# A running maximum, sums and an accumulator of its own for the ninth token set of a soft mixture of experts, and masks kept once

## The chip, the cores and the metric

The kernel runs on 1 core of one Trainium2 chip. The metric is the device time of an execution in microseconds; three runs of the kernel before gave 246.71, 247.36 and 250.5 us, with a median of 247.36 us. PE is the matrix engine (PEld its weight loads), DVE the vector engine, ACT the scalar engine, POOL the GpSimd engine, SP the engine that issues nearly all DMAs.

## The reference

Two parts follow each other. First comes attention over 8 batches, 8 heads, 576 positions and 64 columns per head. Heads 0 to 3 see the last 32 positions ("local"), heads 4 to 7 see every 32nd position ("strided"); the softmax subtracts the row maximum. The result is laid out as `x`, 4608 tokens of 512 columns. Then comes a soft mixture of experts with 8 experts of 4 slots:

```python
logits = x @ phi                                  # 4608 x 32
d = exp(logits - logits.max(0)); d /= d.sum(0) + 1e-9     # over all tokens
slot_input = d.T @ x                              # 32 x 512
slot_out[e] = relu(slot_input[e] @ w1[e]) @ w2[e]
c = exp(logits - logits.max(1)); c /= c.sum(1) + 1e-9     # over the 32 slots
out = c @ slot_out
```

The maximum, the sum and `d.T @ x` over all tokens are built up while attention runs, as running values that are rescaled whenever the maximum moves.

## The kernel before, in words

**Steps.** The work is cut into 16 iterations `i`, one for half the heads of a batch (`i // 2` is the batch). Each iteration takes the same steps, each a small function `emit_...`, named by a short key: scores (SL, SS), masking (a1, aA, a2), maximum and exponential (m, b, EX, s), transposes of the weights (PA, PL, PS), values (AL, AS, AA), normalising (nL, nS, nA), transposes of the result (XL, XS, XB), logits (LG, lc, lg). A table `PHASE` gives each key a time within the iteration, and the sorted list of all times is the order in which the program is written, and so the order on every engine. Keys that end in z stand for the last iteration. Weight loads are sorted into the same list: each takes a buffer when the step that last uses it has been written, and SP issues all loads in that order.

**Sets of tokens.** Tokens 64 to 575 of a batch form one set of 512 tokens, so there are eight sets, one per batch. Logits of such a set are kept as 128 partitions x 128 columns in `lall[:, b, :]`: partition 32 t + slot holds that slot for the t-th quarter of the tokens. Tokens 0 to 63 of all batches form the ninth set. Every fourth iteration (i = 3, 7, 11, 15) has 128 of its tokens together, and writes them to `lall[32 g : 32 g + 32, 8, :]` with g = i // 4.

**The ninth set before.** T9 transposes its 128 tokens (four transposes), x9 copies them, G9 (L577) makes the logits with four matmuls into the 32 partitions of quarter g, c9 copies them to `lall`, b9 takes their maximum, and `first_m9`, `last_m9` fold it into the running negative maximum that all sets share. E9 (L624) takes the exponential on 32 partitions, with the shared maximum; z9 adds its sums to the shared sums `z`. U9 transposes the 32 x 128 result, u9 copies it, and S9 (L675) multiplies it with the tokens: one matmul of 512 columns into the 32 partitions of quarter g of the same PSUM bank that the eighth-part sums SI have just been written to. `ac` (L680) then folds the whole bank into `acc`. In the last iteration SI, S9 and ac are done in two halves of 256 columns.

**The merge.** After the last iteration the four quarters are put together: mt transposes the maximum, gm takes the minimum of the four, wP, wD, wA make a factor per partition, sw scales the stacking matrix, sP (L759) multiplies the accumulator with it, sD (L766) copies the result to `sit`, the slot inputs that the first layer reads. zD, zP, rg make the reciprocal of the sum, which scales the hidden layer. The steps P0 to P6 (`emit_first`, L846) are the first layer and issue weight loads whose buffers it frees. The second layer (`emit_l2`, L944), the coefficients and the output follow.

**Banks.** `take` gives the PSUM bank that has been free the longest, `give` returns it; a step that takes a bank waits until its last reader is done. Engines that touch the same bank are put in order by the program.

**Masks.** `cb` holds the masks of nine score tiles side by side as bf16: four copies of the local mask, one for the first 64 tokens, four copies of the strided mask; 464 columns in all. One DMA at the start (L891) loads it.

Of the kernel before, what the change touches and what calls it, by code (L numbers as in the profile page):

```python
# [50 lines left out]
    lgz=492.0681, c9z=467.7215, bmz=518.3122, zzz=648.0242, z9z=668.8573, dtz=596.2488, EX1z=195.9649, EX2z=170.4399,  # L51
    fAz=234.7687, fLz=274.1149, fSz=217.6755, xLz=423.1816, xSz=473.4095, xBz=528.5387, x9z=397.8597, EDz=528.5407,
    E9z=609.9016, EAz=644.5397, b9=25.0188, U9=26.2638, u9=26.7833, b9z=480.3923, U9z=628.15, u9z=652.4228,
# [44 lines left out]
def tile_sparse_attention_soft_moe(  # L98
# [24 lines left out]
    WM = 320 + 4 * NI  # L123
    cb = big("cb", WM, BF16)
    mask = cb[:, 0:WM]
# [4 lines left out]
    acc = big("acc", 512)  # L130
    d = big("d", 128)
# [156 lines left out]

    def done(name, i, readers):
# [124 lines left out]
    def emit_a(w, i):  # L414

        if i not in box:
            box[i] = [state.tile([P, 9, 2], F32, tag=nm, name=f"{nm}{i}", bufs=4) for nm in ("mx", "rz")]
        s, n, kk, lo, t = {"1": (0, 4, 64, 0, "M1"), "A": (4, 1, 64, 0, "M2"), "2": (5, 4, NI, 128, "M2")}[w]
        dst = psg[2] if w == "2" else psg[1][:, s:s + n]
        mk = mask[:, 320:WM] if w == "2" else mask[:, 64 * s:64 * s + 64 * n]  # L420
# [80 lines left out]
    def emit_nA(i):  # L501
        t, rz = box.pop(("AA", i)), box[i][1]
        r0 = 64 * (i // 2 % 2)
        if i == NQ - 1:
            first_m9(i)
# [71 lines left out]
    def emit_G9(i):  # L577
        t = box["G9", i] = take()
        for c in range(4):
            nc.tensor.matmul(out=t[0][rows9(i), 0:128], lhsT=phs[:, CH[c], :], rhs=xT9(i)[:, c, :],  # L580
                             start=c == 0, stop=c == 3, skip_group_check=True)

    def emit_c9(i):
        r = rows9(i)
        t = box.pop(("G9", i))
        DVE(out=woven(lall[r, B, :]), in_=t[0][r, 0:128].rearrange("p (y k) -> p y k", y=2))
        give(t)

    def first_m9(i):
        st["m9", i] = state.tile([P, 1], F32, tag="m9", name=f"m9_{i}")  # L590
        DVE(out=st["m9", i], in_=st["m", i - 2])

    def emit_b9(i):

        r = rows9(i)
        bm9 = st["bm9", i] = state.tile([P, 1], F32, tag="bm", name=f"bm9_{i}")
        nc.vector.tensor_reduce(out=bm9[r], in_=lall[r, B, :], op=ALU.max, axis=AX.X)
        if i < NQ - 1:
            first_m9(i)
            last_m9(i)  # L600

    def last_m9(i):
        r = rows9(i)
        nc.vector.scalar_tensor_tensor(out=st["m9", i][r], in0=st["bm9", i][r], scalar=-1.0, in1=st["m", i - 2][r], op0=ALU.mult, op1=ALU.min)

    def emit_bm(i):
        b = i // 2
        bm = state.tile([P, 1], F32, tag="bm", name=f"bm{b}")
        nc.vector.tensor_reduce(out=bm, in_=lall[:, b, :], op=ALU.max, axis=AX.X)
        if i == NQ - 1:  # L610
            last_m9(i)

        ngm = st["m", i] = state.tile([P, 1], F32, tag="ngm", name=f"ngm{b}")
        if b == 0:
            nc.vector.tensor_scalar_mul(ngm, bm, -1.0)
        else:
            nc.vector.scalar_tensor_tensor(out=ngm, in0=bm, scalar=-1.0, in1=st["m9" if b % 2 else "m", i if b % 2 else i - 2], op0=ALU.mult, op1=ALU.min)

    def emit_ED(i):
        b = i // 2  # L620
        st["z", i] = state.tile([P, 1], F32, tag="zs", name=f"zs{b}")
        nc.scalar.activation(out=d, in_=lall[:, b, :], func=AF.Exp, bias=st["m", i], accum_out=st["z", i])

    def emit_E9(i):  # L624
        r = rows9(i)
        st["z9", i] = state.tile([P, 1], F32, tag="z9", name=f"z9_{i}")
        nc.scalar.activation(out=d9[r].rearrange("p (y k) -> p y k", y=2), in_=woven(lall[r, B, :]), func=AF.Exp, bias=st["m", i][r], accum_out=st["z9", i][r])
# [11 lines left out]
    def emit_z9(i):  # L639
        r = rows9(i)  # L640
        nc.vector.tensor_tensor(out=st["z", i][r], in0=st["z", i][r], in1=st["z9", i][r], op=ALU.add)
# [10 lines left out]
    def emit_U9(i):  # L652
        t = box["U9", i] = take()
        r = rows9(i)
        nc.tensor.transpose(out=t[0][:, 0:32], in_=d9[r], identity=ident[r, r])
# [19 lines left out]
    def emit_S9(i, hs=(0, 1)):  # L675
        cols = slice(256 * hs[0], 256 * hs[-1] + 256)
        nc.tensor.matmul(out=box["SI", i, hs[0]][0][rows9(i), cols], lhsT=dt9,
                         rhs=x9b[:, cols], start=False, stop=True, skip_group_check=True)
# [22 lines left out]
    for s in "LS":  # L701
# [9 lines left out]
               S9=emit_S9, ac=emit_ac)  # L711
    EVEN, ODD, FOURTH = {"lc", "Dt", "Tt", "et"}, {"lg", "bm", "ED", "EA", "DT", "dt", "SI", "zz", "ac"}, {"T9", "x9", "G9", "c9", "b9", "E9", "z9", "U9", "u9", "S9"}
    HALVES = {"SI", "S9", "ac", "rc"}


    L = NQ - 1
    gm = phs[0:1]
    wg = state.tile([P, 1], F32, name="wg")
    zw = state.tile([P, 1], F32, name="zw")
    rg = state.tile([P, 1], F32, name="rg")  # L720
# [5 lines left out]
    def emit_mt():  # L726
        box["mrg"] = take()
        nc.tensor.transpose(out=box["mrg"][0][0:1, 0:128], in_=st["m", L], identity=ident)
# [9 lines left out]
    def emit_wD():  # L738
        nc.vector.tensor_tensor(out=wg, in0=box["mrg"][0][:, 128:129], in1=st["m", L], op=ALU.subtract)
# [4 lines left out]
    def emit_zD():  # L744
        nc.vector.tensor_tensor(out=zw, in0=st["z", L], in1=wg, op=ALU.mult)

    def emit_zP():
        nc.tensor.matmul(out=box["mrg"][0][:, 129:130], lhsT=same, rhs=zw, start=True, stop=True)

    def emit_rg():  # L750

        nc.vector.tensor_scalar_add(rg, box["mrg"][0][:, 129:130], EPS)
        give(box.pop("mrg"))
        nc.vector.reciprocal(rg, rg)

    def emit_sw():
        nc.vector.tensor_scalar_mul(stw, stack, wg)

    def emit_sP(h):  # L759
        t = box["sit", h] = take()  # L760
        for c in range(2):
            x = 2 * h + c
            nc.tensor.matmul(out=t[0][:, 32 * c:32 * c + 32], lhsT=acc[:, 128 * x:128 * x + 128], rhs=stw,
                             start=True, stop=True, skip_group_check=True)

    def emit_sD(h):  # L766
        t = box.pop(("sit", h))
        DVE(out=sit[:, 2 * h:2 * h + 2, :].rearrange("p c (e x) -> p c e x", x=36)[:, :, :, 0:4],
            in_=t[0][:, 0:64].rearrange("p (c e s) -> p c e s", c=2, e=E))
        give(t)  # L770
# [75 lines left out]
    def emit_first(n):  # L846
# [7 lines left out]
        if n == 1:  # L854
# [4 lines left out]
            "rg": emit_rg, "sw": emit_sw, "ms": lambda: nc.gpsimd.memset(sitb, 0.0), "Px": lambda: ph.append(take())}  # L859
    for h in range(2):  # L860
        once[f"SI{h}"] = lambda h=h: emit_SI(L, (h,))
        once[f"S9{h}"] = lambda h=h: emit_S9(L, (h,))
# [198 lines left out]
```

## Time and profile before

| what | value |
|---|---|
| median of the three runs | 247.36 us |
| the profiled execution | 247.0 us, its span 245.2 us |
| PE busy | 219.2 us, 89% of the span |
| DVE busy | 166.9 us, 68% |
| ACT busy | 155.3 us, 63% |
| POOL busy | 87.3 us, 36% |
| DMA | 72.79 MB, mean 297 GB/s |
| mean granted TensorE clock | 0.967 of full speed |

The profiled execution is 247.0 us long; its span, in which the trace has instructions, is 245.2 us, and 1.8 us lie around it. A line such as L677 is a line of the kernel. In the views, `x32` is a count of instructions. A float32 matmul appears as two PE instructions, a transpose as one.

### The profile page before, as it was taken

Reading aid. Unit: us, or ns where it says so; the run is one execution under the profiler, and the core shown is the slowest. Engines: PE = TensorE matmul, PEld = TensorE weight load, DVE = VectorE, ACT = ScalarE, POOL = GpSimd, SP = SyncE. Lnnn points to the kernel's source line nnn. Section 1 sums busy time; section 2 is a strip of 40 time slices with the busy share of each in tenths; the row PEclk is TensorE's granted clock in tenths of the full one; section 3 lists DMA queues with packets and bytes.
Section 4 is the critical chain, followed back from the end, with each engine's and each line's share of the span. In section 5 each row is a group of like instructions: output and inputs, shape, how many; then the busy total and the mean of one; then the engine's idle time right before and its main releaser. Section 6 shows DMA issues by size and latency. Waiting matters only on the chain.

```text
span 245.2 us, 9712 instructions
## 1 busy us (share of the span) xinstructions
PE 219.2 (89%) x3974; PEld 168.7 (69%) x3974; DVE 166.9 (68%) x378; ACT 155.3 (63%) x344; POOL 87.3 (36%) x187
## 2 busy tenths in 40 slices
PE   6879999999999899999999999997989999898600
PEld 2569889899788789879989988776743245455300
DVE  6077778888779788878998988699767330145800
ACT  2469869797878688797897888694451040134600
POOL 5731662752456177146436603843102000000000
PEclk9799999999999999999999999999999999999955
DMA  6978999999999799999899999796999999988997
GB/s 157 296 225 241 310 301 280 272 295 290 306 278 301 202 318 280 277 276 318 256 289 320 279 258 268 270 266 237 392 413 409 409 398 350 288 282 278 325 364 298
DMA packets 70188, 72.79 MB, mean 297 GB/s; under 512 B 33280, under 2 KB 60288, under 8 KB 70144
## 3 DMA queue, kind: packets, MB, share of 16 engines
q1 hardware_dynamic: 69184, 71.84, 92.4%
q8 instruction: 31, 0.51, 0.9%
q10 hardware_dynamic: 960, 0.33, 0.6%
q14 instruction: 13, 0.11, 0.2%
HBM read 62.72 MB, written 9.44 MB: 294 GB/s over the span
## 4 chain that ended last, share of the span: by engine, by line
PE 67%; DMA 13%; DVE 7%; issue 3%; ACT 2%; SPq 2%; DVEq 0%; ACTq 0%
PE bank L466 11%; PE bank L335 11%; PE bank L385 8%; PE bank L836 6%; PE bank L516 5%; DMA natb<-in_q_dram 5%; PE bank L458 4%; DMA wb<-in_moe_w_dram 4%; PE bank L952 3%; PE bank L671 3%; PE bank L547 3%; DMA natb<-in_k_dram 3%; PE bank L536 2%; PE bank L977 2%; DMA xnb<-in_k_dram 2%
## 5 line engine op out<-in xcount | busy, mean ns | idle before, releaser
L335 PE MATMUL bank<-cf,natb 128*128 128x128 f32 x276 | 40.1, 275 | 1.9 <-DMA natb<-in_q_dram 1.8
L335 PEld LDWEIGHTS bank<-cf,natb 128*128 128x128 f32 x276 | 31.5, 142 | 5.5 <-issue 2.6
L423 DVE TENSOR_TENSOR pb<-bank,cb 128x128 f32<-128x128 f32 (+2 forms) x48 | 22.6, 476 | 9.9 <-PE bank L385 8.4
L351 ACT COPY kLb<-bank 64x256 f32<-64x256 f32 x64 | 25.3, 395 | 3.2 <-PE bank L335 1.3
L496 DVE TENSOR_TENSOR xnb<-bank,rz 128x512 f32<-128x512 f32 (+1 forms) x33 | 21.9, 670 | 7.7 <-ACT ptb L462 2.9
L385 PE MATMUL bank<-kLb,qtb 128*32 128x128 f32 x576 | 24.6, 274 | 1.5 <-ACT kLb L351 0.8
L431 DVE TENSOR_TENSOR pb<-pb,mx 128x288 f32<-128x288 f32 (+1 forms) x32 | 23.1, 722 | 0.7
L428 DVE TENSOR_REDUCE mx<-pb 128x8 f32<-128x288 f32 (+1 forms) x32 | 22.1, 692 | 0.6
L325 POOL COPY vb<-vb 64x1024 f32<-64x1024 f32 x16 | 17.4, 1090 | 14.2 <-PE bank L466 9.8
L438 DVE TENSOR_REDUCE rz<-pb 128x8 f32<-128x288 f32 (+1 forms) x32 | 20.9, 681 | 2.3 <-ACT pb L435 2.0
L435 ACT ACTIVATE pb<-pb 128x288 f32<-128x288 f32 (+1 forms) x32 | 19.0, 598 | 5.5 <-DVE pb L431 5.2
L385 PEld LDWEIGHTS bank<-kLb,qtb 128*32 128x32 f32 x576 | 18.2, 110 | 3.7 <-issue 2.5
L462 ACT COPY ptb<-bank 128x512 f32<-128x512 f32 x32 | 18.8, 590 | 2.9 <-PE bank L458 2.5
L330 POOL COPY natb<-natb 128x512 f32<-128x512 f32 x15 | 9.2, 612 | 31.5 <-DMA natb<-in_q_dram 24.0
L359 ACT COPY kSb<-bank 64x512 f32<-64x512 f32 x32 | 18.6, 581 | 2.3 <-PE bank L335 1.9
L516 PE MATMUL bank<-cf,xnb 128*128 128x128 f32 x128 | 19.8, 278 | 0.1
L378 POOL COPY kLb<-qtb 64x64 f32<-64x64 f32 x32 | 8.6, 267 | 29.9 <-ACT qtb L370 26.4
L466 PE MATMUL bank<-vb,ptb 128*32 128x128 f32 x512 | 18.0, 273 | 0.5 <-issue 0.5
L326 POOL COPY vb<-vb 64x1024 f32<-64x1024 f32 x16 | 18.1, 1129 | 0.7
L458 PE MATMUL bank<-cf,pb 128*128 128x128 f32 x128 | 17.3, 274 | 0.9 <-ACT pb L435 0.8
L466 PE MATMUL bank<-vs,ptb 128*32 128x128 f32 x480 | 17.2, 276 | 0.4 <-ACT ptb L462 0.3
L382 POOL COPY kSb<-qtb 64x32 f32<-64x32 f32 x64 | 16.7, 261 | 2.2
(179 smaller groups left out, 465.9 us busy)
## 6 DMA issues: line engine op xcount, KB each, us to landing
wb<-in_moe_w_dram SPq DMA_DIRECT2D x48, 512.0 KB
natb<-in_q_dram SPq DMA_DIRECT2D x30, 256.0 KB
natb<-in_k_dram SPq DMA_DIRECT2D x30, 256.0 KB
vb<-in_v_dram SPq DMA_DIRECT2D x32, 144.0 KB
vs<-in_v_dram SPq DMA_DIRECT2D x30, 144.0 KB
out_dram<-wb SPq DMA_DIRECT2D x16, 256.0 KB
vb<-in_moe_w_dram SPq DMA_DIRECT2D x4, 512.0 KB
xnb<-in_moe_w_dram SPq DMA_DIRECT2D x3, 512.0 KB
```

The lines of the kernel that those rows point to most:

```text
L335: nc.tensor.transpose(out=t[0][:, 128 * n:128 * n + 128], in_=src[:, 128 * n:128 * n + 128], identity=ident)
L351: ACT(out=dst.rearrange("d (p j n) -> d p j n", j=2, n=2)[:, :, :, n], in_=t[0][64 * n:64 * n + 64].rearrange("d (h j p) -> d p j h", j=2, ...
L385: nc.tensor.matmul(out=t[0][32 * c:32 * c + 32, x:x + wd], lhsT=lhsT, rhs=rhs, start=True, stop=True, skip_group_check=True)
L423: nc.vector.tensor_tensor(out=dst, in0=src, in1=mk.rearrange("p (s k) -> p s k", s=n).unsqueeze(3).to_broadcast([P, n, kk, 2]), op=ALU.add)
L428: nc.vector.tensor_reduce(out=part(box[i][0], w), in_=psg[w].rearrange("p s k a -> p s a k"), op=ALU.max, axis=AX.X)
L431: nc.vector.tensor_tensor(out=psg[w], in0=psg[w], in1=over(box[i][0], w), op=ALU.subtract)
L435: nc.scalar.activation(out=t, in_=t, func=AF.Exp, scale=0.125)
L438: nc.vector.tensor_reduce(out=part(box[i][1], w), in_=psg[w].rearrange("p s k a -> p s a k"), op=ALU.add, axis=AX.X)
L458: nc.tensor.transpose(out=t[0][:, 128 * r:128 * r + 128], in_=pb[:, lo + 128 * r:lo + 128 * r + 128], identity=ident)
L466: nc.tensor.matmul(out=t[0][32 * c:32 * c + 32, 128 * r:128 * r + 128], lhsT=lhsT, rhs=rhs, start=True, stop=True, skip_group_check=True)
L496: nc.vector.tensor_tensor(out=xn[:, place(i, s), r0:r0 + nr].rearrange("p r (a d) -> p r a d", a=2), in0=t[0][:, 128 * r0:128 * r0 + 128 * ...
L516: nc.tensor.transpose(out=t[0][:, 128 * r:128 * r + 128], in_=xn[:, place(i, s), r, :], identity=ident)
```

## The change

The ninth set leaves the shared running values and gets its own: a negative maximum `m9`, sums `z9`, a factor `al9` and an accumulator `acc9` of 128 partitions x 128 columns.

- G9 makes the logits four times, into all four quarters of the bank: 16 matmuls in place of 4.
- b9 takes the maximum straight from the bank, on 128 partitions; E9 takes the exponential straight from the bank too; c9 still copies the 32 partitions to `lall`, and the bank is given back when both c9 and E9 are done. `first_m9` and `last_m9` are gone.
- U9 transposes 128 x 128 in place of 32 x 128.
- S9 takes a bank of its own and makes four matmuls of 128 columns, one per quarter, in place of one of 512 columns; the new step a9 folds it into `acc9`. L9 makes the factor `al9` by an exponential.
- In the last iteration E9, U9 and u9 come before the shared exponential ED, and S9, which was written between the two halves of SI, is written just after the transpose DT.
- In the merge, `mn` is the smaller of the two negative maxima; wD, wA, zD and zP work on two columns; rg has two more small steps; s9w scales the identity by the factor of the ninth set; s9P, written between the two halves of SI, multiplies `acc9` with it into the bank that both halves of sP now add to.
- The masks are kept once (164 columns in place of 464) and repeated by a stride of zero when a1 and a2 read them.

The diff, cut to its core:

```diff
-    ok = np.concatenate([ok_l] * 4 + [ok_a] + [ok_s] * 4, 1)
+    ok = np.concatenate([ok_l, ok_a, ok_s], 1)
...
-        nc.vector.tensor_tensor(out=dst, in0=src,
-                                in1=mk.rearrange("p (s k) -> p s k", s=n).unsqueeze(3).to_broadcast([P, n, kk, 2]), op=ALU.add)
+                                in1=masks[w].unsqueeze(1).unsqueeze(3).to_broadcast([P, n, kk, 2]), op=ALU.add)
...
     def emit_G9(i):
         for c in range(4):
-            nc.tensor.matmul(out=t[0][rows9(i), 0:128], lhsT=phs[:, CH[c], :], rhs=xT9(i)[:, c, :],
+            for f in range(4):
+                nc.tensor.matmul(out=t[0][32 * f:32 * f + 32, 0:128], lhsT=phs[:, CH[c], :], rhs=xT9(i)[:, c, :],
...
     def emit_b9(i):
+        nc.vector.tensor_reduce(out=bm9, in_=box["G9", i][0][:, 0:128], op=ALU.max, axis=AX.X)
+        nc.vector.scalar_tensor_tensor(out=ng, in0=bm9, scalar=-1.0, in1=st["m9", i - 4], op0=ALU.mult, op1=ALU.min)
...
     def emit_bm(i):
+        if i == L:
+            nc.vector.tensor_tensor(out=mn, in0=ngm, in1=st["m9", i], op=ALU.min)
...
     def emit_E9(i):
+        nc.scalar.activation(out=d9, in_=box["G9", i][0][:, 0:128], func=AF.Exp, bias=st["m9", i], accum_out=st["z9", i])
+        done("G9", i, 2)
+    def emit_L9(i):
+        if i > 3:
+            nc.scalar.activation(out=st["al9", i], in_=st["m9", i - 4], func=AF.Exp, bias=st["m9", i], scale=-1.0)
...
-        nc.tensor.transpose(out=t[0][:, 0:32], in_=d9[r], identity=ident[r, r])
+        nc.tensor.transpose(out=t[0][:, 0:128], in_=d9, identity=ident)
...
-    def emit_S9(i, hs=(0, 1)):
-        nc.tensor.matmul(out=box["SI", i, hs[0]][0][rows9(i), cols], lhsT=dt9,
-                         rhs=x9b[:, cols], start=False, stop=True, skip_group_check=True)
+    def emit_S9(i):
+        t = box["S9", i] = take()
+        for f in range(4):
+            nc.tensor.matmul(out=t[0][32 * f:32 * f + 32, 0:128], lhsT=dt9, rhs=x9b[:, 128 * f:128 * f + 128], ...)
+    def emit_a9(i):
+            nc.vector.scalar_tensor_tensor(out=acc9, in0=acc9, scalar=st["al9", i], in1=t[0][:, 0:128], op0=ALU.mult, op1=ALU.add)
...
+    def emit_s9w():
+        nc.vector.tensor_scalar_mul(d9, ident, wg[:, 1:2])
+    def emit_s9P():
+        t = box["sit"] = take()
+        nc.tensor.matmul(out=t[0][:, 0:128], lhsT=acc9, rhs=d9, start=True, stop=False, skip_group_check=True)
     def emit_sP(h):
-        t = box["sit", h] = take()
+        for x in (2 * h, 2 * h + 1):
+            nc.tensor.matmul(out=box["sit"][0][:, 32 * x:32 * x + 32], lhsT=acc[:, 128 * x:128 * x + 128], rhs=stw,
+                             start=False, stop=True, skip_group_check=True)
```

The order of the changed steps in the last iteration, by engine:

```
PE  before: G9 LG XB mt DT wP U9 SI0 S9 SI1 S9 sP0 sP1 P0
PE  after:  G9 LG XB U9 mt DT S9 wP SI0 s9P SI1 sP0 sP1 P0
DVE before: c9 b9 lg bm(last_m9) gm dt wD zz u9 z9 sw ac0 ac1 sD0 sD1
DVE after:  b9 c9 lg bm(mn) u9 gm dt wD a9 zz z9 s9w sw ac0 ac1 sD0 sD1
ACT before: xS xB ED E9 EA wA
ACT after:  xS E9 xB ED EA L9 wA
```

## Rows read from the trace of the kernel before

**Rows 1.** Windows: us, busy us (instructions) per engine, granted clock, DMA share, GB/s.
```profile
20.00:156.00 136.00, 133.67 (x2803) 117.71 (x2805) 113.10 (x251) 112.22 (x252) 65.52 (x143) 1.00 0.96 281
...
171.00:214.00 43.00, 40.95 (x493) 20.69 (x489) 18.70 (x58) 12.00 (x29) 2.90 (x3) 1.00 1.02 383
```
**Rows 2.** The chain that ended last: start us, us, what.
```profile
36.38 0.87 PE bank L385 x32
...
156.05 5.81 DMA natb<-in_q_dram
...
200.90 8.79 DMA wb<-in_moe_w_dram
```
**Rows 3.** Who waited for whom: us in total, times, longest.
```profile
SPq L301 <- PE bank L335: 15.1, 10, 2.6
...
DVE x9b L508 <- PE bank L677: 2.5, 3, 1.0
...
PE bank L952 <- DMA wb<-in_moe_w_dram: 0.9, 1, 0.9
```
**Rows 4.** Window of the weight loads issued ahead of P0, columns as in Rows 1.
```profile
167.09:186.14 19.05, 17.07 (x242) 11.32 (x234) 14.96 (x44) 8.86 (x22) 3.39 (x3) 1.00 0.96 372
```
**Rows 5.** Timeline of SP in that window: first and last of 15 loads.
```profile
167.09 0.43 SPq L262 DMA_DIRECT2D kLb<-in_moe_w_dram  x1
...
181.79 1.24 SPq L256 DMA_DIRECT2D xnb<-in_moe_w_dram  x2
```
**Rows 6.** Timeline of PE around S9 of i = 3: start us, us, engine, line.
```profile
67.28 0.59 PE L677 MATMUL bank<-x9b,dt 128*32 128x512 f32 x1
67.29 0.42 PE L385 MATMUL bank<-kLb,qtb 128*32 128x128 f32 x6
67.71 0.59 PE L677 MATMUL bank<-x9b,dt 128*32 128x512 f32 x1
```
**Rows 7.** Timeline of PE around G9 and U9 of i = 7.
```profile
101.57 0.73 PE L580 MATMUL bank<-xnb,phs 128*32 128x128 f32 x5
...
102.25 0.31 PE L466 MATMUL bank<-vs,ptb 128*32 128x128 f32 x3
...
106.06 0.24 PE L655 MATMUL bank<-cf,d 32*128 32x32 f32 x1
106.23 0.66 PE L335 MATMUL bank<-cf,natb 128*128 128x128 f32 x4
```
**Rows 8.** Groups by form: busy us, mean ns of one | idle before, releasers.
```profile
L385 PEld LDWEIGHTS bank<-kLb,qtb 128*32 128x32 f32 x576 | 18.2, 110 | 3.7 <-issue 2.5 <-ACT kLb L351 1.1
...
L686 DVE SCALAR_TENSOR_TENSOR acc<-acc,al,bank 128x512 f32<-128x512 f32 x6 | 4.5, 746 | 0.2
...
L686 DVE SCALAR_TENSOR_TENSOR acc<-acc,al,bank 128x256 f32<-128x256 f32 x2 | 1.0, 480 | 0.6 <-PE bank L677 0.6
```
**Rows 9.** Timeline of the last iteration and the merge.
```profile
177.17 0.42 DVE L521 COPY xtb<-bank 128x256 f32<-128x256 f32 x1 [1.21 <-ACT xtb L521]
...
178.13 0.30 DVE L586 COPY lall<-bank 32x128 f32<-32x128 f32 x1 [0.54 <-PE bank L580]
...
179.16 0.59 ACT L540 COPY xnb<-bank 128x512 f32<-128x512 f32 x1 [0.77 <-PE bank L536]
...
179.79 0.40 ACT L622 ACTIVATE d<-lall,ngm 128x128 f32<-128x128 f32 x1
180.10 0.19 ACT L622 ACTIVATION_READ_ACCUMULATOR d<-lall,ngm 128x1 f32 x1
...
181.15 0.16 DVE L739 TENSOR_TENSOR wg<-bank,ngm 128x1 f32<-128x1 f32 x1
...
182.24 0.48 DVE L686 SCALAR_TENSOR_TENSOR acc<-acc,al,bank 128x256 f32<-128x256 f32 x1 [0.25 <-PE bank L677]
...
184.20 1.92 PE L836 MATMUL bank<-wb,pb 128*32 128x512 f32 x16
```
**Rows 10.** DMA issues: KB of one.
```profile
cb<-in_cb_dram ACTq DMA_DIRECT2D x1, 116.0 KB
```

More of the change, by code (lines that the diff above doesn't have):

```diff
@@ L121, in big @@
         return const.tile([P, cols], dt, name=nm)
-    WM = 320 + 4 * NI
+    WM = 128 + NI
     cb = big("cb", WM, BF16)
-    mask = cb[:, 0:WM]
+    masks = {"1": cb[:, 0:64], "A": cb[:, 64:128], "2": cb[:, 128:WM]}
     cf = big("cf", 128 + 128 + 32 + 1)
@@ L287, in tile_sparse_attention_soft_moe @@
     st = {}
+    L = NQ - 1
+    mm = state.tile([P, 2], F32, name="mm", bufs=1)
+    zz2 = state.tile([P, 2], F32, name="zz2", bufs=1)
+    mn = state.tile([P, 1], F32, name="mn", bufs=1)
     def done(name, i, readers):
@@ L579, in emit_G9 @@
         for c in range(4):
-            nc.tensor.matmul(out=t[0][rows9(i), 0:128], lhsT=phs[:, CH[c], :], rhs=xT9(i)[:, c, :],
-                             start=c == 0, stop=c == 3, skip_group_check=True)
+            for f in range(4):
+                nc.tensor.matmul(out=t[0][32 * f:32 * f + 32, 0:128], lhsT=phs[:, CH[c], :], rhs=xT9(i)[:, c, :],
+                                 start=c == 0, stop=c == 3, skip_group_check=True)
     def emit_c9(i):
         r = rows9(i)
[L585 to L591, printed above, removed]
-    def emit_b9(i):
[L595 to L604, printed above, removed]
+        DVE(out=woven(lall[r, B, :]), in_=box["G9", i][0][r, 0:128].rearrange("p (y k) -> p y k", y=2))
+        done("G9", i, 2)
+    def emit_b9(i):
+        bm9 = state.tile([P, 1], F32, tag="bm", name=f"bm9_{i}")
+        nc.vector.tensor_reduce(out=bm9, in_=box["G9", i][0][:, 0:128], op=ALU.max, axis=AX.X)
+        ng = st["m9", i] = mm[:, 1:2] if i == L else state.tile([P, 1], F32, tag="m9", name=f"m9_{i}")
+        if i == 3:
+            nc.vector.tensor_scalar_mul(ng, bm9, -1.0)
+        else:
+            nc.vector.scalar_tensor_tensor(out=ng, in0=bm9, scalar=-1.0, in1=st["m9", i - 4], op0=ALU.mult, op1=ALU.min)
     def emit_bm(i):
@@ L609, in emit_bm @@
         nc.vector.tensor_reduce(out=bm, in_=lall[:, b, :], op=ALU.max, axis=AX.X)
-        if i == NQ - 1:
-            last_m9(i)
-        ngm = st["m", i] = state.tile([P, 1], F32, tag="ngm", name=f"ngm{b}")
+        ngm = st["m", i] = mm[:, 0:1] if i == L else state.tile([P, 1], F32, tag="ngm", name=f"ngm{b}")
         if b == 0:
@@ L639, in emit_z9 @@
     def emit_z9(i):
[L640 to L641 removed]
+        if i > 3:
+            nc.vector.scalar_tensor_tensor(out=st["z9", i], in0=st["z9", i - 4], scalar=st["al9", i], in1=st["z9", i],
+                                           op0=ALU.mult, op1=ALU.add)
     def emit_DT(i):
@@ L727, in emit_mt @@
         box["mrg"] = take()
-        nc.tensor.transpose(out=box["mrg"][0][0:1, 0:128], in_=st["m", L], identity=ident)
+        nc.tensor.transpose(out=box["mrg"][0][0:1, 0:128], in_=mn, identity=ident)
     def emit_gm():
@@ L744, in emit_zD @@
     def emit_zD():
-        nc.vector.tensor_tensor(out=zw, in0=st["z", L], in1=wg, op=ALU.mult)
+        nc.vector.tensor_tensor(out=zw, in0=zz2, in1=wg, op=ALU.mult)
     def emit_zP():
-        nc.tensor.matmul(out=box["mrg"][0][:, 129:130], lhsT=same, rhs=zw, start=True, stop=True)
+        nc.tensor.matmul(out=box["mrg"][0][:, 129:131], lhsT=same, rhs=zw, start=True, stop=True)
     def emit_rg():
-        nc.vector.tensor_scalar_add(rg, box["mrg"][0][:, 129:130], EPS)
+        DVE(out=zw, in_=box["mrg"][0][:, 129:131])
         give(box.pop("mrg"))
+        nc.vector.scalar_tensor_tensor(out=rg, in0=zw[:, 1:2], scalar=0.25, in1=zw[:, 0:1], op0=ALU.mult, op1=ALU.add)
+        nc.vector.tensor_scalar_add(rg, rg, EPS)
         nc.vector.reciprocal(rg, rg)
     def emit_sw():
-        nc.vector.tensor_scalar_mul(stw, stack, wg)
-    def emit_sP(h):
-        t = box["sit", h] = take()
[L761 to L764, printed above, removed]
+        nc.vector.tensor_scalar_mul(stw, stack, wg[:, 0:1])
+    def emit_s9w():
[3 more added lines that the diff above has]
+        nc.tensor.matmul(out=t[0][:, 0:128], lhsT=acc9, rhs=d9, start=True, stop=False, skip_group_check=True)
+    def emit_sP(h):
+        for x in (2 * h, 2 * h + 1):
+            nc.tensor.matmul(out=box["sit"][0][:, 32 * x:32 * x + 32], lhsT=acc[:, 128 * x:128 * x + 128], rhs=stw,
+                             start=False, stop=True, skip_group_check=True)
     def emit_sD(h):
-        t = box.pop(("sit", h))
         DVE(out=sit[:, 2 * h:2 * h + 2, :].rearrange("p c (e x) -> p c e x", x=36)[:, :, :, 0:4],
-            in_=t[0][:, 0:64].rearrange("p (c e s) -> p c e s", c=2, e=E))
-        give(t)
+            in_=box["sit"][0][:, 64 * h:64 * h + 64].rearrange("p (c e s) -> p c e s", c=2, e=E))
+        if h:
+            give(box.pop("sit"))
     CSETS = ((0, 4), (4, 7), (7, NV))
@@ L858, in tile_sparse_attention_soft_moe @@
     once = {"zv": emit_zv, "mt": emit_mt, "gm": emit_gm, "wP": emit_wP, "wD": emit_wD, "wA": emit_wA, "zD": emit_zD, "zP": emit_zP,
-            "rg": emit_rg, "sw": emit_sw, "ms": lambda: nc.gpsimd.memset(sitb, 0.0), "Px": lambda: ph.append(take())}
+            "rg": emit_rg, "sw": emit_sw, "s9w": emit_s9w, "s9P": emit_s9P, "ms": lambda: nc.gpsimd.memset(sitb, 0.0), "Px": lambda: ph.append(take())}
     for h in range(2):
         once[f"SI{h}"] = lambda h=h: emit_SI(L, (h,))
-        once[f"S9{h}"] = lambda h=h: emit_S9(L, (h,))
         once[f"ac{h}"] = lambda h=h: emit_ac(L, (h,))
```

48 lines of the change are left out of this document (25 added, 23 removed).

## The prediction

> **What bounds the kernel now.** I read the windows first, to see which engine is full in which stretch. From 20 to 156 us, the attention loop, PE is busy 133.67 of 136 us and the DMA engines have a share of 0.96 [rows 1]: two resources are full at once, and DVE and ACT, at 113.1 and 112.2 us, have 17% to spare. From 171 to 214 us the DMA share is 1.02: the weights stream in without a gap. The chain of waits says how the two are coupled. In the loop it is nearly all PE; it then goes through a query load issued at 156.05 that lands 5.81 us later, and in the second layer through a weight load issued at 200.90 that takes 8.79 us [rows 2]. The list of waits says which way the coupling goes. SP waited 15.1 us, ten times, for PE to free a buffer at L335: loads of attention are issued at PE's pace. In the second layer PE stood still 0.9 us for a weight load [rows 3]: there, PE arrives before the weights.
>
> How far ahead the weight loads are decides what the merge may cost. Between 167.09 and 186.14, when the first load behind P0 is issued, 15 loads are issued [rows 5], each of 128 x 1024 float32 values or 0.524 MB: 7.86 MB. 19.05 us at 372 GB/s moved 7.09 MB [rows 4], some of it value loads issued before. So at least 0.77 MB are outstanding, 2.1 us at that rate. P0 can start later by about that much before the stream of weights runs dry.
>
> **The change on PE, in the loop (i = 3, 7, 11).** S9 was two passes, started 0.43 us apart, so 0.86 us in one quarter of the array; six passes of other work ran beside the first [rows 6]. A pass of 128 columns that shares the array with three others costs 0.87 / 32 = 0.027 us [rows 2], so that the cover is worth 6 x 0.027 = 0.16 us, somewhat more in the other two sets: the old S9 cost about 0.64 us. The new one is 8 passes in four quarters, 8 x 0.027 = 0.22 us. Gain 0.42 us. G9 had 8 passes in one quarter at 0.107 (four times 0.027), 0.86 us, with about five other passes beside it [rows 7], net 0.72; the new 32 passes cost 0.87 us and leave no quarter for others: a loss of 0.14 us. U9 held PE from 106.06 to 106.23, 0.17 us [rows 7]; as a full transpose like those of L335, 0.66 us less a tail for four, it takes 0.11 (one pass) to 0.17: gain 0.03. Together 0.3 us for a set, 0.9 us for three. The bounds are 0 (the DMA share of 0.96 sets the pace, and PE only waits longer) and 0.9. I take 0.7, nearer to the PE end, because SP's 15.1 us of waiting were for PE.
>
> Here rows and the Trainium skill differ. A row of the chain has 32 passes with full contraction and 32 columns of weights in 0.87 us [rows 2], and each has a weight load of its own of 110 ns, 3.5 us if they ran one after another [rows 8]. So loads of different column groups overlap. The Trainium skill, "TensorE: Matmul & The Clock Gate", Part 3, "The mechanism", says that a weight load overlaps matmuls in flight only when its row group differs, and all these loads use all rows. By that rule the 24 additional loads of G9 would stand in the open; the row decides against it, and it is the last rival below.
>
> **DVE and ACT in the loop.** A set loses `first_m9` and its shared `last_m9` and gains `m9`, a9 and a wider z9. The accumulating operation takes 746 ns for 512 columns and 480 for 256 [rows 8], 1.04 ns a column, so a9 at 128 columns is 0.35 us; a tiny operation takes 0.16 [rows 9]. Balance: +0.35 + 0.16 + 0.06 - 2 x 0.15, about +0.27 us a set, 0.8 us in all. What hides it: right there DVE waited for S9 before it could overwrite the tokens, 2.5 us in three times [rows 3], and S9 now ends earlier. If that cover fails, up to 0.8 us. L9, an exponential of one column, puts at most ED's 0.40 us [rows 9] on ACT in two of the sets, ahead of the copies of the key transposes: between 0 and 0.8; I take 0, since the shared maximum ahead of ED is ready one small operation earlier. G9's bank is held until E9 and S9 takes one more. By the order of takes and gives the bank that E9 frees goes to DT, which waits for ED anyway, two steps of PE's queue later: nothing, unless ACT falls behind, and then E9's 0.40 us.
>
> **Masks.** The load shrinks from 116 KB [rows 10] to 164 / 464 of it, 75 KB less; at the mean of 297 GB/s that is 0.25 us of the first loads, of which a part is on the chain. Between 0 and 0.25, I take 0.1. The same number of mask elements is read as before; nothing for the stride of zero, with a bound of some tens of ns on 48 operations that DVE's spare 17% would take up.
>
> **The merge.** Here the change adds waits. Two engines that read disjoint halves of one bank go one after the other: DVE waited 1.21 us until ACT was done with the other half [rows 9]. E9 now reads the bank of G9 as c9 does, so E9 stands behind c9. b9 starts where c9 did, at 178.13; with b9 0.28, m9 0.16 and c9 0.30 and the gaps, c9 ends at 178.9. E9 with its accumulator read takes 0.40 + 0.19 [rows 9], to 179.5; behind it on ACT are the 0.59 us copy xB, which started at 179.16 before, and ED, which started at 179.79 and now starts at 180.15. Waiting for ED: DT, and on PE's queue behind DT also S9 and wP, and so wD, which moves from 181.15 to 181.5. Then DVE has a9 (0.35) and s9w (0.35, priced as a9) in place of u9 (0.18): ac0 moves from 182.24 to about 183.1. s9P stands on PE ahead of the second half of SI and waits for s9w, so ac1 follows to 184.2. The first sD must wait until the second sP has written into the same bank. From the first ac's end at 182.72 to P0 at 184.20 lay 1.48 us, with both sP, an sD and the second ac in them; from the second ac's end, sP and sD alone take an estimated 1.0 of these. P0 starts at about 185.2 in place of 184.20 [rows 9]: +1.0 us. Bounds: +0.1 (nothing but the added operations, if bank order costs nothing) and +1.4 (every added operation at its longest, with a gap behind each).
>
> Of the 1.0 us, PE's stand of 0.9 us in the second layer [rows 3] takes up 0.9, and the outstanding 2.1 us of loads keep the stream from running dry. If loads need part of that lead to flow, some is lost again: between 0 and 1.0 I take 0.3.
>
> **Sum**, against the profiled execution of 247.0 us (its span of 245.2 and 1.8 around it): -0.7 - 0.1 + 0 + 0.3 = -0.5, so 246.5 us. The median of the runs shown is 0.36 above that execution: 247.36 - 0.5 = 246.9 us. A change of 2%, about what a measurement of this kernel can tell from no change, would be 5 us.
>
> **Rivals.**
> 1. All of the gain arrives: PE's 0.9 us a loop and the masks' 0.25, with the merge fully hidden: -1.15, and some 0.3 more where an earlier load meets a freer DMA queue: 246.0. For it: the waits of SP for PE. Against it: a DMA share of 0.96.
> 2. The merge becomes the bound. The stream of weights has only 2.1 us in hand when P0 issues its loads; what a load needs from its issue to a steady flow no row shows, and between 0 and 2.1 us of that lead may go into it. If it is all of it, P0 at +1.0 leaves a hole of 1 us, all later loads move with it, and PE's stand in the second layer grows instead of hiding anything. It decides from the point where P0's delay and that start together exceed 2.1 us. With a DMA-bound loop (no gain): +1.0 to +1.4, 248.5. For it: the load behind that wait is the last step on the chain before the output. Against it: the share of 1.02 over the whole stretch.
> 3. S9 does not do what it says: its four matmuls run one after another at 0.107 a pass, 0.86 us, and with G9's loss each set is 0.36 us slower: +1.1, with the merge 248.7. Against it: the 32 passes in 0.87 us.
> 4. Weight loads don't overlap: 24 more for G9 and 6 for S9, 30 x 0.110 = 3.3 us a set, +9.9 in three: 257. Against it: the same row.
>
> **Chances.** Forecast 0.50 (its own range 246.2 to 247.8), rival 1 0.22, rival 2 0.20, rival 3 0.05, rival 4 0.01, and 0.02 for a faster loop that I can't name. The likeliest is 246.9. The range reaches into rival 1 and to rivals 2 and 3 with the spread of the runs: 245.3 to 248.7. Only rival 4, and rival 2 or 3 together with every upper bound, reach 2%: slower 0.03, faster 0.02, the rest within.
>
> **What would show it.** S9's passes in groups of four within some 0.25 us, G9's 32 in 0.87 (rivals 3 and 4 otherwise); the wait of DVE at L508 shorter; the last query load of the loop issued 0.5 to 0.9 us before 156.05; ED at about 180.15 less that gain, behind E9 and xB; P0 about 1.0 us later against G9 of the last iteration; PE's stand of 0.9 us in the second layer gone or smaller; the DMA share at 1.02 throughout. Wrong would be a first weight load of the tail (167.09) that is not earlier, a dip of the DMA rate near 186, or a longer stand in the second layer.

## The result, and the profile after

The changed kernel takes 246.05 us (median of 20 runs) against 249.52 us for the kernel before on the same chip (20 runs): a ratio of 0.9895, with a 95% interval of 0.9855 to 0.9935. Ratios with an interval, here and below, compare the fast runs of two kernels alone (those within 1.5% of the fastest of the same kernel), so they differ from the ratio of the two medians printed beside them. That is 2.6 us less, between 1.6 and 3.6. The forecast was 246.9 us, or 0.5 us less, a ratio of 0.998: the time lies in the range, the sign is right, and the step is larger than the forecast one by more than the measurement is uncertain. That 246.05 lies so near 246.9 is luck: the forecast took off from the median of three runs, 247.36 us, and from the 249.52 us of twenty runs the same step would have given 249.0.

The profiled execution of the changed kernel took 247.91 us (span 246.1), above the median of its runs; that of before, 247.0, is below the median of 249.52. So the two spans say nothing against each other; the lengths of single stretches do.

Windows of the kernel after, columns as in [rows 1]: the loop, the first 6 us of the first layer (from P0), the last 14 us.

```profile
20.00:156.00 136.00, 130.28 (x2891) 116.53 (x2881) 115.10 (x251) 111.61 (x254) 64.17 (x140) 1.00 0.93 284
...
186.30:192.30 6.00, 6.00 (x54) 1.91 (x58) 4.17 (x10) 1.15 (x2) 1.85 (x2) 1.00 0.91 347
...
232.10:246.10 14.00, 1.13 (x14) 0.69 (x12) 2.33 (x4) 1.76 (x4) 0.00 (x0) 0.68 0.97 360
```

In the loop the DMA engines now move 284 GB/s with a share of 0.93; before, 281 GB/s took a share of 0.96 [rows 1]. The same bytes cost less DMA time, and nothing in the forecast would do that. The first 6 us of the first layer in the kernel before, and its end, where only the output is left to be written:

```profile
184.20:190.20 6.00, 6.00 (x55) 1.91 (x58) 4.32 (x10) 1.15 (x2) 1.85 (x2) 1.00 1.03 409
...
231.20:245.20 14.00, 0.00 (x0) 0.00 (x0) 0.54 (x1) 0.08 (x1) 0.00 (x0) 0.55 0.91 333
```

From P0 the weights flow at 347 GB/s after, at 409 before. At the end the kernel before wrote at 333 GB/s; after writes at 360, the second sight of a change in the transfers. The last group of output matmuls, first of before, then of after (start us, us, engine, line):

```profile
223.25 7.28 PE L977 MATMUL bank<-x9b,lall 32*128 32x256 f32 x96 [0.35 <-ACT x9b L968]
```
```profile
225.95 7.28 PE L990 MATMUL bank<-x9b,lall 32*128 32x256 f32 x96 [0.35 <-ACT x9b L981]
```

The same matmuls in the same 7.28 us; from their end to the end of the span (245.2 and 246.1) it is 14.67 us before and 12.87 us after. These 1.8 us are most of the 2.6.

The steps of the ninth set itself, in the timeline of PE after: U9 and S9 of i = 3, then G9 of i = 7 (compare [rows 6, 7]).

```profile
65.99 0.27 PE L654 MATMUL bank<-cf,d 128*128 128x128 f32 x1
66.10 0.60 PE L341 MATMUL bank<-cf,natb 128*128 128x128 f32 x4
...
69.16 0.40 PE L677 MATMUL bank<-x9b,dt 128*32 128x128 f32 x8
69.37 1.06 PE L391 MATMUL bank<-kLb,qtb 128*32 128x128 f32 x32
...
102.48 1.08 PE L584 MATMUL bank<-xnb,phs 128*32 128x128 f32 x32
103.38 0.84 PE L471 MATMUL bank<-vs,ptb 128*32 128x128 f32 x24
```

U9 holds PE for 0.11 us, the eight passes of S9 for 0.21, the 32 of G9 for 0.90.

The merge, first G9 of the kernel before, then the steps of after (timeline, to be laid beside [rows 9]):

```profile
177.04 0.73 PE L580 MATMUL bank<-natb,phs 128*32 128x128 f32 x5
```
```profile
178.25 1.08 PE L584 MATMUL bank<-natb,phs 128*32 128x128 f32 x32
...
179.72 0.16 DVE L599 SCALAR_TENSOR_TENSOR mm<-bm,m 128x1 f32<-128x1 f32 x1
179.90 0.30 DVE L589 COPY lall<-bank 32x128 f32<-32x128 f32 x1
...
180.29 0.37 ACT L620 ACTIVATE d<-bank,mm 128x128 f32<-128x128 f32 x1 [0.69 <-DVE lall L589]
...
181.11 0.41 ACT L616 ACTIVATE d<-lall,mm 128x128 f32<-128x128 f32 x1
...
183.63 0.47 DVE L694 SCALAR_TENSOR_TENSOR acc<-acc,al,bank 128x256 f32<-128x256 f32 x1
...
186.30 1.06 PE L850 MATMUL bank<-wb,pb 128*32 128x512 f32 x8 [0.38 <-DVE pb L781]
```

ACT was idle for 0.69 us before E9 (L620). E9 takes the maximum m9 (L599), which was done at 179.88; from then on it stood 0.41 us more, until c9 (L589), a reader of the same bank on another engine, was done, as forecast. From the start of G9 to P0 (L850) it is 8.05 us; before, from 177.04 to 184.20, it was 7.16.

Waits of the kernel after (us, times, longest), beside [rows 3]:

```profile
SPq L307 <- PE bank L341: 15.1, 10, 3.0
...
DVE x9b L511 <- PE bank L471: 3.2, 5, 1.5
...
PE bank L965 <- DMA wb<-in_moe_w_dram: 1.5, 1, 1.5
```

SP waits as much for PE as before; DVE waits before the copy of the tokens no longer for S9; PE's stand in the second layer is 1.5 us, where it was 0.9.

### The profile page after: what moved, and what is told of

Read it like the earlier page. It is cut to its first block, busy times and chain, and to the rows that moved or that the text cites. A ratio compares the mean times of both kernels' runs of the same rounds, so it can differ in the third digit from the quotient of the medians.

```text
span 246.1 us, 9961 instructions
## 1 busy us (share of the span) xinstructions
PE 217.3 (88%) x4094; PEld 169.0 (69%) x4094; DVE 168.6 (68%) x381; ACT 154.6 (63%) x347; POOL 87.2 (35%) x187
## 4 chain that ended last, share of the span: by engine, by line
PE 72%; DMA 8%; DVE 6%; issue 4%; ACT 3%; SPq 0%; DVEq 0%; ACTq 0%
PE bank L471 12%; PE bank L341 12%; PE bank L391 10%; PE bank L519 6%; PE bank L850 5%; PE bank L463 5%; DMA wb<-in_moe_w_dram 4%; PE bank L965 3%; PE bank L539 3%; PE bank L550 2%; PE bank L670 2%; DMA vs<-in_v_dram 2%; PE bank L990 2%; DMA natb<-in_q_dram 2%; ACT kLb L357 2%
## 5 line engine op out<-in xcount | busy, mean ns | idle before, releaser
L341 PE MATMUL bank<-cf,natb 128*128 128x128 f32 x276 | 40.7, 278 | 4.6 <-issue 2.2
L341 PEld LDWEIGHTS bank<-cf,natb 128*128 128x128 f32 x276 | 32.1, 143 | 8.1 <-issue 6.5
L391 PE MATMUL bank<-kLb,qtb 128*32 128x128 f32 x576 | 23.1, 273 | 1.5 <-ACT kLb L357 0.8
L436 DVE TENSOR_TENSOR pb<-pb,mx 128x288 f32<-128x288 f32 (+1 forms) x32 | 23.8, 743 | 0.7
L391 PEld LDWEIGHTS bank<-kLb,qtb 128*32 128x32 f32 x576 | 17.6, 110 | 2.7 <-issue 1.6
L519 PEld LDWEIGHTS bank<-cf,xnb 128*128 128x128 f32 x128 | 14.3, 141 | 4.0 <-issue 2.0
L471 PE MATMUL bank<-vs,ptb 128*32 128x128 f32 x480 | 16.1, 275 | 0.7 <-DMA vs<-in_v_dram 0.4
```

Source lines behind the costliest of these rows:

```text
L341: nc.tensor.transpose(out=t[0][:, 128 * n:128 * n + 128], in_=src[:, 128 * n:128 * n + 128], identity=ident)
L391: nc.tensor.matmul(out=t[0][32 * c:32 * c + 32, x:x + wd], lhsT=lhsT, rhs=rhs, start=True, stop=True, skip_group_check=True)
L436: nc.vector.tensor_tensor(out=psg[w], in0=psg[w], in1=over(box[i][0], w), op=ALU.subtract)
L471: nc.tensor.matmul(out=t[0][32 * c:32 * c + 32, 128 * r:128 * r + 128], lhsT=lhsT, rhs=rhs, start=True, stop=True, skip_group_check=True)
L519: nc.tensor.transpose(out=t[0][:, 128 * r:128 * r + 128], in_=xn[:, place(i, s), r, :], identity=ident)
```

## The experiments

Two theories. **Theory A** is the prediction's: the gain is PE's time in the loop, moderated by the DMA. **Theory D** came from the DMA share: `cb` is the first tile that the kernel puts in SBUF. With tiles rounded up to 32 bytes a partition, 928 bytes of masks have become 352, and `acc9` (512 bytes) has been added among the same constant tiles: 576 less and 512 more, so every large buffer that DMA fills or empties has moved down by 64 bytes. In the program as built, `natb` began at byte 27456 of its partition, 64 past a multiple of 256, and the other load and output buffers likewise; now it is 27392, a multiple of 256, and so are they. The first runs were chosen before theory D stood.

**The masks alone.** The kernel before, with the masks kept once and nothing else; by the sizes above `natb` then begins at 26880, a multiple of 256 too.

```diff
-    ok = np.concatenate([ok_l] * 4 + [ok_a] + [ok_s] * 4, 1)
+    ok = np.concatenate([ok_l, ok_a, ok_s], 1)
...
-                                in1=mk.rearrange("p (s k) -> p s k", s=n).unsqueeze(3).to_broadcast([P, n, kk, 2]), op=ALU.add)
+                                in1=masks[w].unsqueeze(1).unsqueeze(3).to_broadcast([P, n, kk, 2]), op=ALU.add)
```

> The kernel before with one part of the change alone: the masks kept once (41 KB loaded at the start in place of 116). The changed kernel has a ratio of 0.9895 to the kernel before. Theory A (the gain comes from PE's work for the ninth set in the loop): the masks give 0 to 0.25 us, ratio 0.999 to 1.000. Theory B (the gain comes from the start, where the first loads land earlier and everything after them moves): most of the 2.6 us, ratio 0.990 to 0.992. Theory C (the gain comes from taking E9, U9 and S9 out of the end of the merge): 1.000.

Measured: 245.49 us against 248.62, ratio 0.9937, 0.9888 to 0.9986. Faster by 1.6 us (0.3 to 2.8), where a load that is 75 KB shorter was to give 0 to 0.25. Its last 14 us:

```profile
227.90:241.90 14.00, 1.14 (x14) 0.70 (x12) 2.35 (x4) 1.77 (x4) 0.00 (x0) 0.70 0.97 360
```

It writes the output at 360 GB/s, as after does.

**Less PE work alone.** The kernel before, with S9 cut to 128 of its 512 columns for i = 3, 7, 11 (three quarters of the ninth set's sum are left out there).

```diff
     def emit_S9(i, hs=(0, 1)):
+        if i < NQ - 1:
+            cols = slice(0, 128)
```

> The kernel before, with S9 cut to its first 128 of 512 columns in the sets of i = 3, 7 and 11; the sums of the ninth set leave out the other three quarters of the columns there. PE loses 0.64 us of single-quarter passes in each, 1.9 us in all, less some 0.5 us of other passes that ran beside them: 1.4. Theory A: the ratio is 0.994 to 0.996, since most of PE's gain arrives. Theories B and C, and a loop paced by the DMA: 0.999 to 1.001.

Measured: 248.54 against 248.62, ratio 0.9991, 0.9924 to 1.0057. No gain is seen; the interval would still hide the 1.4 us that were expected.

**More PE work.** The kernel after, with G9 computed twice, and in a second run five times, for i = 3, 7, 11.

```diff
+        for again in range(2 if i < L else 1):    # second run: 5
+            for c in range(4):
+                for f in range(4):
...
```

> The changed kernel with the 16 matmuls of G9 written twice in the sets of i = 3, 7 and 11 (the second time gives the same numbers). This adds 0.87 us to PE three times, 2.6 us, and nothing else. Theory A, PE sets the pace of the loop: 2.0 to 2.6 us longer than the changed kernel, ratio to the kernel before 0.9975 to 1.000. A loop paced by the DMA: the added time is taken up, ratio 0.9895 as without it.

> The changed kernel with G9 written five times in the sets of i = 3, 7 and 11: 3.5 us more of PE three times, 10.4 us in all, in sets that last some 40 us each. If PE set the pace of the loop (Theory A), 9 to 10.4 us longer than the changed kernel: ratio to the kernel before 1.026 to 1.032. If the DMA sets it and PE has the slack that its waits show (about 4 us of 153 in the loop), 4 to 6 us longer: 1.006 to 1.014.

Measured: twice, 247.17 against 248.62, ratio 0.9986 (0.9925 to 1.0047), which is 0.9% above the changed kernel's 0.9895, give or take 0.7%, for 2.6 us, 1.0%, of passes. Five times: four runs of 254.13 to 260.03 us, median 258.69 against 249.27, too few for an interval. They can be laid beside the changed kernel's twenty runs: the lowest is 11.6 us above the lowest there (242.51), the highest 9.8 us above the highest (250.2), for 12 x 0.87 = 10.4 us of passes. In the profiled execution the stretch from the first scores to G9 of the last iteration is 176.7 us long; in the other eight kernels with buffers at multiples of 256 it is 163.0 to 166.8. Its loop:

```profile
20.00:156.00 136.00, 131.00 (x3082) 118.18 (x3080) 105.39 (x232) 102.93 (x235) 61.66 (x133) 1.00 0.87 263
```

PE stays full and the DMA share falls to 0.87. Of 10.4 us of work added to PE, about all arrives, so with that much more of it PE does bound the loop; that work taken away gives as much back is not shown by it.

**The merge, another order.** The kernel after, with c9, z9 and the sums zz late, ED ahead of xB, and s9P just behind the second half of SI (it stood ahead of it).

```diff
-    s9P=730.2656, c9z=480.3923, zzz=648.0242, z9z=648.1, EDz=528.5407
+    s9P=730.2757, c9z=731.2, zzz=731.0, z9z=731.1, EDz=528.5
```

> The changed kernel with five times of the last iteration moved, no work added or left out: ED ahead of the copy xB on ACT, c9 and the sums zz and z9 behind the last sD on DVE, s9P behind the second half of SI on PE. P0 should start 1.0 to 1.5 us earlier against G9 than in the changed kernel (where it starts 8.0 us after G9, against 7.1 in the kernel before). If the merge is hidden under the stream of weights, as the prediction has it, the ratio stays at 0.9895. If P0 comes so late that the stream of weights has a hole (rival 2 of the prediction; the DMA share was 0.98 and the rate dipped to 353 GB/s in one slice after 185 us), the time falls by 0.5 to 1.2 us, to 0.985 to 0.9875.

Measured: 243.18 against 248.62, ratio 0.9887, 0.9833 to 0.9942. From G9 to P0 it is 6.84 us in place of 8.05. With c9 late, E9 waits for m9 alone (G9 starts at 177.51 here), 1.73 us behind G9 in place of 2.04: c9's place in the bank is worth 0.31 us. And from P0 the weights flow without the dip:

```profile
179.24 0.37 ACT L620 ACTIVATE d<-bank,mm 128x128 f32<-128x128 f32 x1 [0.38 <-DVE mm L599]
```
```profile
184.35:190.35 6.00, 6.00 (x54) 1.91 (x58) 4.82 (x13) 1.15 (x2) 1.84 (x2) 1.00 1.01 400
```

But its list of waits has a longer stand of PE for weights in the second layer, 1.8 us, where after has 1.5 and before 0.9, and the ratio is that of the changed kernel: part of the earlier P0 is paid back in waiting.

**The addresses alone.** The kernel before, doing the same work: a small tile of 128 bytes is moved to another part of SBUF and 64 bytes of padding are put ahead of the buffers, so that they begin at multiples of 256 (three one-word tiles keep a single copy, to make room).

```diff
-    dt, dt9 = big("dt", 128), big("dt9", 32)
+    dt, dt9 = big("dt", 128), state.tile([P, 32], F32, name="dt9", bufs=1)
+    big("pad", 16)
```

> The kernel before, same work, same order, masks four times; only the place of the buffers in SBUF is moved. In the kernel before every buffer that a large DMA writes or reads (natb, kLb, vb, xnb, the weight buffers and so on) begins 64 bytes behind a multiple of 256 in each partition; in the changed kernel and with the masks alone kept once, all begin at a multiple of 256. Here the small tile dt9 is put elsewhere, so that they all begin 64 bytes earlier, at the same addresses as in the changed kernel. Theory D (what the smaller mask tile is worth is the addresses that it gives to the buffers behind it): the last 16 us move 363 GB/s in place of 334, the time from the last output matmul to the end is 12.9 us in place of 14.5, and the ratio is 0.992 to 0.994, as with the masks alone. Theory B (the 75 KB not loaded at the start): 1.000 and 334 GB/s.

Measured: 244.93 against 249.27, ratio 0.979, 0.9727 to 0.9853. A kernel that computes exactly what before computes is 2% faster (1.3% when it ran again on another chip, below).

**The changed kernel without them.** 64 bytes of padding put its buffers back to 64 past a multiple of 256.

```diff
+    big("pad", 16)
...
-    wac = state.tile([P, 1], F32, name="wac")
+    wac = state.tile([P, 1], F32, name="wac", bufs=1)
```

> The changed kernel, with 64 unused bytes put ahead of natb, so that every buffer behind begins where it did in the kernel before, 64 bytes past a multiple of 256. Theory D: the end goes back to 334 GB/s and 14.5 us, and the ratio to the kernel before is 0.996 to 0.999, what is left of the gain without the addresses. Theory A (PE's work in the loop): 0.9895, as without the pad. Theory B: 0.9895.

Measured: 249.01 against 249.27, ratio 0.9987, 0.9946 to 1.0029. The gain is gone. The last output matmuls, first with the addresses alone, then with the changed kernel moved back:

```profile
220.46 7.28 PE L978 MATMUL bank<-x9b,lall 32*128 32x256 f32 x96 [0.36 <-ACT x9b L969]
```
```profile
227.87 7.28 PE L991 MATMUL bank<-x9b,lall 32*128 32x256 f32 x96 [0.35 <-ACT x9b L982]
```

and the windows of the last 14 us, in the same order:

```profile
226.60:240.60 14.00, 1.14 (x14) 0.70 (x12) 2.35 (x4) 1.77 (x4) 0.00 (x0) 0.63 0.97 360
```
```profile
235.90:249.90 14.00, 0.00 (x0) 0.00 (x0) 0.45 (x1) 0.00 (x0) 0.00 (x0) 0.59 0.92 333
```

From the end of the matmuls to the end of the span (240.6 and 249.9): 12.86 and 14.75 us. The rate and the 1.9 us go with the addresses, whichever kernel they are in. Theories B (the shorter load at the start) and C (less at the end of the merge) of the first expectation fall with these two runs: the kernel moved back has the shorter load and the new merge and gains nothing, the one with the addresses alone has neither and gains all.

**Three kernels side by side.** The kernel after as it is, before with moved buffers, and the other merge order, on one chip.

> The changed kernel itself, beside the next two on one chip, so that the three can be compared with the same runs of the kernel before. Theory D (all of the gain is the place of the buffers, the ninth set's own work is worth nothing): the same time as the kernel before with its buffers moved by 64 bytes, within 0.5%. If the changed work in the loop gains 0.7 us and the merge loses 0.3, as predicted, 0.4 us (0.2%) less than that one; if the later P0 leaves a hole in the stream of weights, 0.5 to 1.5 us (0.2 to 0.6%) more.

> The kernel before with its buffers moved by 64 bytes to multiples of 256, the same kernel as in e6, now beside the changed kernel. Measured on another chip: 0.979 of the kernel before (0.973 to 0.985). Theory D: 0.979 to 0.990, and equal to the changed kernel within 0.5%.

> The changed kernel with the order of the merge moved, the same kernel as in e4, now beside the changed kernel. P0 is 1.2 us earlier against G9 in it. If the merge is hidden behind the stream of weights: equal to the changed kernel within 0.3%. If the later P0 costs anything: 0.5 to 1.2 us (0.2 to 0.5%) faster than the changed kernel, and then the fastest of the three.

Measured, against 249.55: 244.94, ratio 0.9805 (0.9736 to 0.9874); 245.35, 0.9868 (0.9811 to 0.9924); 243.37, 0.977 (0.9707 to 0.9832). The intervals overlap, and with buffers at multiples of 256 the kernel with the old work is as fast as the one with the new: beside the addresses, neither the ninth set's new work nor the merge order can be told from nothing. The other merge order had the lowest median in both of its comparisons, 243.2 and 243.4 us (the changed kernel itself ran beside it in the second alone); it beats the kernel before, and is not shown to beat the changed one.

**Other offsets.** The kernel after with its buffers at 128 and at 192 bytes past a multiple of 256 (in the second, `wac` keeps a single copy, as above).

```diff
-    dt, dt9 = big("dt", 128), big("dt9", 32)
+    dt, dt9 = big("dt", 128), state.tile([P, 32], F32, name="dt9", bufs=1)
+    big("pad", 16)     # second run only
```

> The changed kernel with dt9 put elsewhere, so that the buffers behind begin 128 bytes past a multiple of 256 (0 in the changed kernel, 64 in the kernel before). If any start off a multiple of 256 costs the same: 334 GB/s in the last 16 us and a ratio near 0.999, as with 64 bytes. If what costs is bytes fetched below the start, more with a larger offset: less than 334 GB/s, some 325, and a ratio above 1.000. If only a multiple of 128 is wanted: 363 GB/s and 0.980 to 0.990.

> The same with the buffers 192 bytes past a multiple of 256. If any offset costs the same: 334 GB/s and near 0.999. If the cost grows with the offset: the lowest rate of all, some 315 GB/s, and 1.005 to 1.010.

Measured, against 250.56: 249.59, ratio 0.9976 (0.9911 to 1.0041), and 249.91 (too few runs for an interval). The last 14 us of the first and of the second:

```profile
233.30:247.30 14.00, 0.00 (x0) 0.00 (x0) 0.47 (x1) 0.01 (x1) 0.00 (x0) 0.58 0.92 334
```
```profile
232.70:246.70 14.00, 0.00 (x0) 0.00 (x0) 0.27 (x1) 0.00 (x0) 0.00 (x0) 0.61 0.93 333
```

Every offset tried costs the same in the rate; in the time of the whole kernel a difference between them would hardly show.

The main queue's line on the page (packets, MB, share of 16 engines) says it for the whole kernel, before and after:

```profile
q1 hardware_dynamic: 69184, 71.84, 92.4%
```
```profile
q1 hardware_dynamic: 69184, 71.84, 89.7%
```

Packets and bytes are the same. Share times span is 226.6 us before and 220.8 after. Over all profiled kernels it is 225.5 to 228.2 us in the five with an offset, and 219.9 to 222.4 in the nine without, the one with 10 us of added PE work among them. Of the 5.8 us between before and after, the writes of the output hold 0.8 (26.6 and 25.8 us, added up from the trace's packets); the other 5 lie in loads. How much of those reaches the end through the loop, where the DMA share is 0.93 to 0.96, was not separated: from the first scores to G9 of the last iteration, the five kernels with an offset took 164.9 to 168.0 us, the eight others (without the one with 10 us of added work) 163.0 to 166.8.

## Why the prediction was right in sign, and for another reason

**The masks: the step that failed.** "The load shrinks ... 75 KB less ... I take 0.1" counted what the edit saves in itself. What it did was to shift all buffers behind the masks. The term was put at -0.1 with a lower bound of -0.25; the masks alone measured -1.6 us (0.6% faster, 0.1 to 1.1), and the shift alone as much as the whole change or more (0.979 and 0.9868 against 0.9895 and 0.9805). The new `acc9` belongs to the same step: 576 bytes less and 512 more give 64, just what was missing. That was luck, and with it the sign: with the buffers at 64, 128 or 192 bytes past a multiple of 256 the changed kernel is not measurably faster than the one before (smaller shifts were not tried). The other half of that step holds: the mask additions took 475 ns in the mean after, 476 before, so the stride of zero costs nothing.

**PE in the loop: prices right, effect not seen.** Forecast and found: S9 0.22 and 0.21 us, G9 0.87 and 0.90, U9 0.11 to 0.17 and 0.11. Rival 3 (S9's matmuls one after another) and rival 4 (weight loads in the open) are refuted by the same rows. The sum of -0.7 us is not confirmed: the changed kernel with the old offset has 0.9987 (0.9946 to 1.0029), which holds the forecast of 0.998 and holds no change too. SP's 15.1 us of waiting for PE, on which the 0.7 rested, are unchanged.

**DVE and ACT.** a9 takes 0.34 us (0.35 forecast), and DVE no longer waits for S9 before it copies tokens. That nothing of DVE's 2 us more in the loop, 115.10 against 113.10, reaches the end can't be told from a small gain that cancels it.

**The merge: +0.9 us for +1.0.** 7.16 us have become 8.05. The way there was partly another: ED starts 2.86 us after G9 in place of 2.75, so it lost 0.1 and not 0.36, and ac0 5.38 in place of 5.20, 0.2 later where 0.9 was forecast; the rest arises behind it. So the sum is right and its terms are not. E9's wait behind c9 was there as forecast, 0.41 us in the trace, and worth 0.31 us when c9 was moved. The Trainium skill, "PSUM — Partial Sum Buffer", section "PSUM bank collisions raise a hardware error", has it that two engines, readers too, must not be in one bank and the same partitions at once, and that the compiler adds a dependency; the order of the two readers in this trace agrees.

**Hidden or not: 0.3 us was probably too little.** Two signs of rival 2 are there. The dip is one: in the first 6 us from P0 the DMA moved 184 to 348 GB/s in all seven executions with this merge, 371 to 409 in the five with the old one, and 400 and 421 in the two with the other order. The longer stand is the other, 1.5 us for 0.9, so that the point "PE's stand gone or smaller" was wrong in this execution; in the second one of the same kernel (the three kernels side by side) it was 0.3 us, so the stand tells little. From G9 of the last iteration to the first write of the output, where the granted clock was full throughout, it took 38.4 to 40.5 us with this merge (four executions), 37.4 to 38.2 with the old one (four), 38.2 and 38.5 with the other order. This points to about 1 us, the size of rival 2, and not to 0.3. The times don't settle it: the ratios of the other order, 0.9887 and 0.977, lie beside 0.9895 and 0.9805, and 1 us is below what these runs resolve, about 1%.

The forecast also left out the clock. In the other three of the seven executions with this merge the granted clock fell to 0.50 (1.2 GHz) near P0, for 3.4 to 6.8 us; in none of the other seven did it fall there. In the second execution of the changed kernel it fell at 181.0 us, after 3 us in which PE was busy for 2.16, and P0 came 9.42 us after G9 in place of 8.05. That the longer merge is the cause is not shown.

**The queries.** The last query load was issued at 157.53, not before 156.05; the first scores of that execution started 1.0 us later too (12.67 against 11.64), and the loop, from its first to its last score matmul, took 153.5 us against 153.3. The first weight load of the tail came at 167.11, not before 167.09, which the prediction had named as a sign of being wrong. The forecast 0.5 to 0.9 us are not there; between executions of one kernel this stretch differs by more (152.3 us in the second one of the changed kernel).

## What to carry to other kernels

A change in the size of any tile moves every tile behind it; where DMA buffers lie behind it, look at their start modulo 256 bytes before and after, and pad to a multiple. To put them first would not be enough here: the first tile, `cb`, starts at byte 16512, which is 128 past one. When a kernel gets faster and its engines don't, compare DMA share with GB/s in the same window: the same bytes at less share is a change in the transfers. Where the queue is full all the time, as at the end here, the GB/s alone tell. A control that computes nothing new and only moves memory (0.979 here) is cheap, and says which part of a gain belongs to the edit.

## What was not expected of the hardware

Buffers whose start in the partition is a multiple of 256 bytes are written out at 358 to 361 GB/s over the last 14 us (nine kernels); with starts 64, 128 or 192 bytes past it, at 333 to 334 (five). The kernel gains 1 to 2% by it. Those 14 us mix two things: the first two thirds of the output go out in rows of 1 KB, the last third in rows of 2 KB, and the last 1.2 us hold no transfer. A window within each kind, of before, then of after:

```profile
228.00:235.00 7.00, 2.53 (x34) 1.56 (x28) 3.74 (x7) 3.04 (x6) 0.00 (x0) 0.82 1.00 340
236.50:242.50 6.00, 0.00 (x0) 0.00 (x0) 0.00 (x0) 0.00 (x0) 0.00 (x0) 0.50 1.02 382
```
```profile
229.00:236.00 7.00, 4.23 (x58) 2.80 (x52) 5.43 (x10) 4.51 (x9) 0.00 (x0) 1.00 1.09 383
238.50:243.50 5.00, 0.00 (x0) 0.00 (x0) 0.00 (x0) 0.00 (x0) 0.00 (x0) 0.50 1.05 406
```

The changed kernel at 64, 128 and 192 bytes has 341, 341 and 340 GB/s in rows of 1 KB, 382, 383 and 383 in rows of 2 KB. So a row of 1 KB takes 13% longer and a row of 2 KB 6%, whatever the offset: about the same time for each row. The Trainium skill, "DMA: Bandwidth & Descriptors", section "How a descriptor splits into AXI transactions", says that a transaction must start at a 256-byte boundary, and that a descriptor which doesn't start there begins with one from the boundary below, whose unused bytes still cost beats. The boundary of 256 agrees with these runs. By its count of beats a row of 2 KB would cost an estimated 66, 68 and 70 beats for 64 at the three offsets, 3, 6 and 9%, and a row of 1 KB an estimated 34, 36 and 38 for 32, 6, 13 and 19%. Measured are 6 and 13% at each: the count agrees at 128 bytes and not at 64 and 192, and the measurement decides. Why the cost doesn't grow with the offset stays open, and what it is for loads was not measured by itself.
